# The MLP's down product by Strassen's scheme in a fused RWKV-7 and gelu MLP kernel

## The chip, the cores and the metric

One core of one Trainium2 chip. The metric is device time in microseconds for one execution. Engines are named as in the profile: PE (TensorE's matmuls, PEld its weight loads), DVE (VectorE), ACT (ScalarE), POOL (GpSimd), SP (the queue that issues the DMAs).

## The reference

A linear attention (RWKV-7) over 4 batches, 8 heads, 768 steps and 40 channels gives x of 3072 tokens by 320; behind it stands an MLP with a hidden width of 2048. All in float32 (the MLP's weights come as float64).

```python
for t in range(S):
    y[:, :, t] = np.einsum('bhd,bhde->bhe', rt, state)
    Sa = np.einsum('bhde,bhe->bhd', state, at)
    state_decay = state * wt[:, :, None, :] - np.einsum('bhd,bhe->bhde', Sa, bt)
    state = state_decay + np.einsum('bhd,bhe->bhde', vt, kt)
...
h = x @ w_in                              # 3072 x 320 by 320 x 2048
g = h * (1.0 / (1.0 + np.exp(-1.702 * h)))
return (g @ w_out).astype(np.float32)     # 3072 x 2048 by 2048 x 320
```

## The kernel before

Time is cut into 12 chunks of 64 steps. A chunk has two **units** (each for two of the four batches), 24 in all. A unit's attention is done in chunk form: decays (`decay`), scores (`prep`), the inverse of a triangular matrix in five doubling steps (`inverse`), and the state's read-out and update (`solve`). A step of the inverse goes from PE (`ps_level`) to DVE, which makes E (line 765) and transposes it to ES (line 714), then to ACT, DVE or POOL, which spread ES to EX (lines 719, 721), and back to PE; ACT or DVE copy W out of PSUM beside it (line 763). A unit ends with the decayed read-out "x" (`decayed`, line 965: four multiplies of 128x128 on DVE or POOL) and a way through DRAM that turns it into xT.

When both units of a chunk are done, the chunk's **MLP** (`mlp`) works on its 256 tokens: four quarters q of `up` matmuls (64x256, ps_up), each followed by a `gelu` on ACT (line 1000) that writes the tile g (4 buffers), and two `down` products (p = 0, 1; 128 tokens each) that add up all 16 blocks of the hidden width in one PSUM pair (64x320, ps_down). `store` copies one PSUM bank to ob (ACT or DVE, line 1024), adds the other (DVE, line 1026) and stores. PSUM is four pairs of banks, shared by everything. Every matmul works on a 64x64 quarter of PE's array, and four quarters are in work at once. The weights are turned from float64 to float32 on chip at the start, with a tile `extra` for raw pieces, free afterwards; POOL adds the halves in `joined` (line 475).

The order of everything is a list, `ORDER` (line 109): each token is a task's number, the engine's letter (p, a, d, g, s) and the PSUM pair. `Plan.add` notes what each task must follow, `Plan.listed` reads the list, and each engine works its tasks strictly in that order. Which engine makes an EX, an "x" or a copy is settled there too. In the list as it is, the MLP's matmuls fill PE's queue between the attention's, and lag behind the attention by one to two chunks (xT has three buffers).

Of the kernel before, what the change touches and what calls it, by code (L numbers as in the profile page):

```python
# [58 lines left out]
class Plan:  # L59
# [5 lines left out]
    def add(self, rank, engines, fn, reads=(), uses=(), writes=(), room=(), pair=None, most=None, size=0, release=0.0):  # L65

        t = Task(rank, engines, fn, pair, most, size)
        t.release = release  # L70
        for key in uses:
            self.used.setdefault(key, []).append(t)
        for key in reads:
            t.after.update(self.made[key])
            self.used.setdefault(key, []).append(t)
        for name, n in (*writes, *room):
            if name in self.slots:
                old = (name, n - self.slots[name])
                t.after.update(self.made.get(old, ()), self.used.get(old, ()))
        for key in writes:  # L80
            self.made.setdefault(key, []).append(t)
        if pair is not None:
            writers = self.of_pair.setdefault(pair, [])
            t.after.update(o for o in writers if "PE" in o.engines)
            writers.append(t)
        t.after.discard(t)
        self.tasks.append(t)
# [22 lines left out]
0s 8s 1s4 5s 102a 7s 6s 3a 9s 158a 87p0 88p1 10s 89a1 100p2 90a0 95d 13s4 4a 11s 93d 12s 101d2 98p3 2s 94d 97d 17s 103p1 16s  # L110
96d 143p0 15s 104a1 105d1 142p2 144a0 106d 99d3 107p1 145a2 18s4 149g 132p3 108a1 109d1 156p0 45s4 150d 27s 151g 157d0 159p2
14s4 110p1 160a2 161d2 91s4 130p0 162d 19a 24s4 112d1 163p2 111a1 22d 26s4 25s 164a2 113p1 20d 131a0 153g 165d2 34s4 92a 274s
21d 166p0 114a1 152g 273s 148a 154p2 115d1 275s 167a0 168d0 116p1 23g 28a 155d2 264p0 345s 117d1 265p2 133a3 344s 266a2 118d1
169p3 36s 31d 33s 119p1 278g 170a3 171d3 35s 120d1 42s 122a1 172p2 279d 280g 121a 43s 124d1 123a1 126p3 174d2 125a1 127d3 287a
29d 128p1 173a2 44s4 288p3 30d 54s4 37a 175p2 129d1 32g 51s4 290d3 134p1 179a2 147s4 176d2 146s 267a0 135d1 177a 188p0 291d
136p1 277s4 180a2 268g 61s 38d 189a0 343s 289a3 182p0 39d 186p3 138a1 40d 137a1 178a2 292p1 315d 181a2 139d 183a0 53s4 282g
276s 187a3 184p2 294d1 140s 283p0 293a1 335p3 281d 41g 185d2 334p1 284d0 190p2 336a3 60s4 347s 316p0 191d2 318a0 348d 357a
192p3 349d 317d0 358p2 194a3 346s2 62s 193d3 295p0 337a1 195g 360d2 46a 285p3 361d 319p1 296a0 297d0 351g 320a1 286d3 362p0
196s 271a 350d 141s 352g 298p1 338d 363a0 364d0 321p3 385d 359a2 299a1 300d1 386p0 323p2 197s4 49d 322a3 301p1 387a0 47d 324a2
63s4 365p3 302a1 303d1 325d2 388a0 304p1 366a3 367d3 355p0 353p2 308a1 48d 269s3 209p3 52s3 309a1 307d1 210p3 50g 270s3 64a  # L120
305d1 211p3 354d2 212p3 213p3 356d0 310a1 198p2 306a 214p3 65d 199p2 215p3 72s3 216p3 70s3 272d 55a 311p1 339s3 200p2 69s4
368p0 312a1 66d 201p2 369a0 202p2 58d 470p1 203p2 370d0 471a 475s 204p2 478s 205p2 67d 389p0 479s 472a1 492d 206p2 68g 482s
341a 207p2 371p1 390d0 208a2 217p3 373d1 220p0 221p0 56d 474s4 218p3 485g 71s4 222p0 219a3 473d 81s4 223p0 484d 79s 313p2
224p0 372a1 225p0 226p0 314d2 227p0 342d 374p3 231p1 480s4 378a3 232p1 57d 380a3 326p2 562s4 379a3 59g 228p0 78s4 377a3 327d2
233p1 73a 234p1 229p0 375d3 328p2 376d 230a0 391p3 486g 481s3 329d2 340s4 242p0 531d 392a3 483g 330d2 381p3 235p1 382a3 331d
236p1 393p2 487g 243p0 558s4 394d2 80s4 244p0 395d2 74d 488p3 237p1 489d3 532p2 238p1 75d 533a2 383p3 239p1 534a2 332s4 384d3
240p1 76d 493p2 396p3 496a2 495d2 77g 241a1 245p0 397d3 82a 490p1 559s3 398p3 491d1 476a 560s4 83d 333s 253p1 494d2 497d 254p1
84d 85d 255p1 400d3 86g 561s4 550p2 246p0 705s 399d3 551a 572d 555s 247p0 498d 552a2 554s 401d 499a 256p1 553g 556a 500p3 566d
402s 570p2 567g 501a3 248p0 571d2 502d3 565g 249p0 564d 696p2 563g 257p1 250a0 403s2 251d0 477d 258p1 252s 535p3 259p1 536a3
557d 697a 573p0 537p3 575d0 260p1 576a0 700s4 503d 698a2 611d 504g 538a3 539p2 574d0 261a1 578d 568p3 540a2 704s 404p0 577g  # L130
569d3 579a 405p0 406p0 541d2 787s3 702a 407p0 708s 710d 408p0 580p3 409p0 582d3 410p0 262d1 612p2 411p0 583d 711g 412p0 613d2
413p0 614d2 505p1 709d 584g 414a0 426p2 427p2 506d1 706s2 428p2 507d1 429p2 699d 430p2 581d3 615p1 703d 431p2 616a1 585p0
432p2 586a0 508d 433p2 587d0 434p2 509a 784s2 588d 435p2 589d 448p3 436a2 510p1 590p0 511a1 449p3 592d0 591a0 512d1 263s2
415p2 513d 701s 416p2 593d 514a 785s 417p2 594g 418p2 515p0 419p2 516a0 517d0 595p1 518d 420p2 596a1 597d1 421p2 598d 422p2
519a 599d 423p2 424p2 520p0 425a2 437p1 521d0 438p1 523d0 522g 439p1 524d0 440p1 525d0 441p1 442p1 526d0 527p2 718p0 528a2
443p1 719d0 929s 444p1 720d0 529p2 445p1 721d0 446p1 530d2 600p0 723d 447a1 542p2 722d 724g 603d0 605a0 619p1 604d0 543d2
450p3 620a1 606d0 544p2 621d1 601d0 602d 617p1 707s 546d2 451p3 618a1 783s 712d 547g 713d 607p0 725p1 608a0 452p3 609p0 453p3
548s 610d0 932s 454p3 727d1 726d1 622p0 728d 545d2 729a 775p1 455p3 623d0 780s 776a 549s 756d 730p2 624p0 456d3 457d3 731d2
458s 459p3 777a1 778g 732d2 786s 788g 781a 779s 626d0 460p3 625d0 627g 733d 795p1 835d 734a 461p3 735p2 791g 462p3 628s 736a2
796d1 737d2 716p0 792g 738d 463p3 782d 739g 1011s 920p1 757p2 925s 464p3 717d0 758a2 629s 759a2 790d 465p3 740p0 789d 466p3  # L140
741a0 742d0 921a 797p2 467d3 760p0 1008s 468d3 800a2 923d 652p3 469s 761d0 922a1 653p3 926a 930s 798d2 714p1 799d2 654p3 924s
802d 801g 655p3 934d 803a 656p3 836p0 657p3 715d1 658p3 659p3 837d0 762p2 838d0 927d 660p3 763a2 661p3 764p1 662a3 743d 630p0
744d 928s 631p0 632p0 765d1 804p2 766d1 633p0 805a2 806d2 634p0 807d 635p0 808a 745p3 636p0 748d3 637p0 749d3 839p1 933g 750d3
638p0 840a1 1009s 751d3 639p0 809p2 746d3 935g 640a0 641p1 810d2 642p1 793p3 747a 811d2 674p0 812d 794d3 813a 752p2 643p1
753a2 814p3 644p1 815a3 816d3 754p2 645p1 755d2 646p1 817d 647p1 818a 767p3 841p2 768d3 648p1 842a2 649p1 819p3 650p1 820a3
821d3 769p2 822d 651a1 823d 675p0 771d2 931s 770d2 772g 824p3 936d 676p0 827a3 828a3 942p1 829a3 677p0 1153s 830a3 937d 945a1
773s 663p2 825d3 664p2 943d1 1156s 826a 665p2 944d1 999p3 947d 946g 666p2 1000a 1004s 980d 940p1 948g 667p2 941d1 668p2 774s
669p2 670p2 831p1 671p2 1001a3 1002d 1003s 832d1 672p2 1005a 1013d 678p0 673a2 1006d 833p3 843p1 679p0 834d3 1007s 844d1 938p3
845d1 680p0 939d3 846p2 681p0 847d2 949p1 1012g 682d0 848p3 950a1 683d0 1014d 684s 685p2 849d3 1015g 1010s 850d3 1021p0 1016g
951d1 686p2 1024a0 1232s 851d 1235s 981p3 687p2 982a3 952d 852s 1022d0 983a3 953g 1144p1 1023d0 688p2 1026d 1145a 1149s 1025d  # L150
1027g 984p3 1059d 689p2 1154s 954p0 853s 985a3 1147g 690p2 1158d 1148s 955a0 956d0 986p3 1146a1 957d 1150a 691p2 958d 987a3
1151d 988p0 692p2 989a0 1152s 990d0 959p1 693a2 865p3 960a1 694d2 866p3 961d1 867p3 695s 962d 868p3 963d 1028p0 869p3 1029a0
1030d0 870p3 1031d 1157g 871p3 1159d 1032a 1060p2 872p3 873p3 1061a2 874p3 1062d2 1033p1 875a3 854p0 1035d1 855p0 1036d 856p0
1037d 1063p2 857p0 1064d2 1034a1 858p0 964p3 859p0 965a3 966d3 1038p1 967d 860p0 1039a1 1040d1 861p0 1041d 1017p2 968a 1042g
862p0 1018d2 863p0 969p3 864a0 876p1 970d3 877p1 972d3 971g 1043p2 973d3 878p1 1044a2 974d3 879p1 975d3 880p1 881p1 1045d2
1019p0 1046d 976p3 1047a 882p1 1020d0 1233s 883p1 977a3 1166p2 884p1 1169a2 1167d2 1377s 978p0 885p1 1168d2 898p3 1171d 1170g
886a1 979d0 887p2 1172a 1048p0 991p1 1051a0 888p2 1052a0 992d1 889p2 1053a0 890p2 1054a0 891p2 1049d0 993p1 1050a 1067p0 994d1
# [94 lines left out]
def rwkv7_gelu_quick(ctx: ExitStack, tc: tile.TileContext, time_d, v_d, w_d, wc_d, ak_d, b_d, rv_d, w_in, w_out, out):  # L252
    nc = tc.nc
    H, D, S = 8, 40, out.shape[0] // 4
    DM = H * D
# [731 lines left out]
    def mlp(c):  # L987
# [47 lines left out]
        for p in BITS:  # L1035
            down(p)
# [105 lines left out]
```

## Time and profile before

| | |
|---|---|
| median of 3 runs (lowest to highest) | 682.02 us (680.43 to 682.2) |
| profiled execution, span from first to last instruction | 680.9 us |
| mean granted clock of TensorE | 0.987 (0.79 between 20 and 60 us, else 1.00) |
| matmul records, all / ps_up / ps_down | 19488 / 3840 / 3072 |
| gelu on ACT | 48 of 1024 ns |
| DVE instructions | 912 |
| POOL instructions | 204 |

The profiled execution's time is shown as its span only; one of the runs is shorter than it, so next to nothing lies around it. Busy time of an engine is the union of its instructions' durations. A matmul of float32 stands in the trace as two records, each with a weight load. Group lines give line, engine, operation, tiles (out<-in), count, then durations or busy time; timeline lines give start, length of the merged piece, engine, line, operation and count, so neighbouring pieces' starts give the pace. Wait lines give who waited for whom, the total in us, how often, and the longest.

### The profile page before, as it was taken

What the parts mean: (1) busy time and instruction counts of PE and PEld (TensorE: products, weight loads), DVE (VectorE), ACT (ScalarE), POOL (GpSimd) and SP (SyncE); (2) the same over time, 40 slices, a digit from 0 to 9 for tenths busy, and PEclk for the clock granted to TensorE, in tenths of its full rate; (3) what the DMA queues carried; (4) which work ended last, traced back from release to release, by engine and by line L of the source; (5) the groups of instructions that cost most, each with busy time, mean ns of one, the idle gap of its engine ahead of it and who ended that gap; (6) DMA issues with size and microseconds to landing.
All of it is one profiled execution on the core that took longest, in us unless ns stands there. A gap on an engine that the chain in (4) does not pass through costs nothing.

```text
span 680.9 us, 42186 instructions
## 1 busy us (share of the span) xinstructions
PE 651.5 (96%) x19488; PEld 561.8 (83%) x19488; DVE 452.8 (66%) x912; ACT 328.9 (48%) x682; POOL 175.4 (26%) x204
## 2 busy tenths in 40 slices
PE   5677999999999999999999999999999999999997
PEld 4666998787999788888888898798888799898785
DVE  5686789767867758858776687768666766675001
ACT  3665845644554754574445455455354354262110
POOL 5442345224123223223213221222412320300000
PEclk9977999999999999999999999999999999999999
DMA  7875563415314414432404513513412411200100
GB/s 218 275 245 148 180 203 110 142 42 152 110 36 130 129 33 120 125 115 71 126 13 126 150 38 108 153 35 106 145 33 70 121 53 42 73 13 23 51 12 20
DMA packets 35312, 69.73 MB, mean 102 GB/s; under 512 B 5440, under 2 KB 14656, under 8 KB 35136
## 3 DMA queue, kind: packets, MB, share of 16 engines
q1 hardware_dynamic: 35136, 67.03, 32.7%
q8 instruction: 153, 2.51, 1.5%
q14 instruction: 23, 0.19, 0.1%
HBM read 59.15 MB, written 7.86 MB: 98 GB/s over the span
## 4 chain that ended last, share of the span: by engine, by line
PE 90%; DMA 5%; DVE 2%; ACT 1%; issue 1%; SPq 1%; ACTq 0%; DVEq 0%
PE ps_up L303 30%; PE ps_down L303 30%; PE ps_level L303 8%; PE ps_y L303 5%; PE ps_B L303 4%; PE ps_X L303 3%; PE ps_N L303 2%; PE ps_rz L303 1%; PE ps_RV L303 1%; PE ps_A L303 1%; DMA w_sb<-in_w_in 1%; PE ps_zT L303 1%; PE ps_cum L303 1%; DMA rv<-in_rv 1%; DMA b<-in_b 1%
## 5 line engine op out<-in xcount | busy, mean ns | idle before, releaser
L303 PE MATMUL ps_up<-xT_all,w_sb 64*64 64x256 f32 x3840 | 249.4, 377 | 0.2 <-PE ps_rz L303 0.2
L303 PE MATMUL ps_down<-w_sb,g 64*64 64x320 f32 x3072 | 239.7, 430 | 0.2 <-ACT zr L881 0.2
L303 PEld LDWEIGHTS ps_up<-xT_all,w_sb 64*64 64x64 f32 x3840 | 168.3, 133 | 15.7 <-PE ps_rz L303 0.3
L303 PEld LDWEIGHTS ps_down<-w_sb,g 64*64 64x64 f32 x3072 | 135.5, 133 | 36.7 <-ACT zr L881 0.4
L1000 ACT ACTIVATE g<-ps_up 128x1024 f32<-128x1024 f32 x48 | 49.2, 1024 | 46.1 <-PE ps_up L303 45.6
L721 POOL TENSOR_TENSOR EX<-ES,quads 128x512 f32<-128x512 f32 x30 | 39.7, 1325 | 118.2 <-DVE ES L714 78.4
L763 ACT COPY W<-ps_level 128x512 f32<-128x512 f32 x56 | 32.7, 585 | 66.8 <-PE ps_level L303 65.2
L303 PEld LDWEIGHTS ps_level<-W,EX 64*64 64x64 f32 x2560 | 57.7, 134 | 6.2 <-DVE T L842 0.2
L765 DVE TENSOR_TENSOR E<-two,ps_level 128x256 f32<-128x256 f32 x80 | 33.1, 415 | 34.4 <-ACT W L763 29.7
L303 PE MATMUL ps_level<-W,EX 64*64 64x64 f32 (+1 forms) x2560 | 54.6, 217 | 0.0
L719 ACT ACTIVATE EX<-ES,quads 128x256 f32<-128x256 f32 x82 | 37.2, 501 | 31.7 <-DVE ES L714 31.3
L303 PEld LDWEIGHTS ps_level<-PT,EX 64*64 64x64 f32 x1280 | 32.0, 144 | 12.0 <-DVE EX L735 3.5
L631 POOL TENSOR_TENSOR ak<-ak,FT 128x512 f32<-128x512 f32 x17 | 22.1, 1299 | 76.7 <-DMA ak<-in_ak 49.8
L303 PE MATMUL ps_level<-PT,EX 64*64 64x64 f32 (+2 forms) x1280 | 34.0, 240 | 7.4 <-DVE EX L735 5.0
L714 DVE STREAM_TRANSPOSE ES<-E 128x256 f32<-128x256 f32 x80 | 35.3, 443 | 4.4
L303 PE MATMUL ps_y<-M,bh 64*64 64x104 f32 (+1 forms) x768 | 35.9, 252 | 1.1 <-issue 0.8
L303 PE MATMUL ps_y<-RV,kh 64*64 64x104 f32 (+1 forms) x768 | 36.2, 253 | 0.7 <-DVE M L919 0.5
L903 ACT COPY B<-ps_B 128x416 f32<-128x416 f32 (+1 forms) x35 | 17.2, 492 | 33.4 <-PE ps_B L303 33.2
L303 PEld LDWEIGHTS ps_y<-RV,kh 64*64 64x64 f32 x768 | 29.2, 137 | 3.2 <-DVE M L919 1.3
L919 DVE TENSOR_TENSOR M<-ps_X,later 128x832 f32<-128x832 f32 (+1 forms) x24 | 23.9, 994 | 11.3 <-PE ps_X L303 10.5
L303 PEld LDWEIGHTS ps_y<-M,bh 64*64 64x64 f32 x768 | 27.8, 137 | 1.8 <-issue 1.2
L303 PE MATMUL ps_B<-RV,A 64*64 64x104 f32 (+1 forms) x768 | 28.5, 250 | 0.4 <-issue 0.3
(133 smaller groups left out, 1085.3 us busy)
## 6 DMA issues: line engine op xcount, KB each, us to landing
ak<-in_ak SPq DMA_DIRECT2D x48, 160.0 KB
rv<-in_rv SPq DMA_DIRECT2D x48, 160.0 KB
time<-in_time SPq DMA_DIRECT2D x24, 320.0 KB
xT_all<-x_dram SPq DMA_DIRECT2D x48, 160.0 KB
wc<-in_wc SPq DMA_DIRECT2D x20, 264.0 KB
logw<-in_w SPq DMA_DIRECT2D x24, 160.0 KB
RV<-in_v SPq DMA_DIRECT2D x24, 160.0 KB
b<-in_b SPq DMA_DIRECT2D x48, 80.0 KB
```

Source lines behind the costliest of these rows:

```text
L303: nc.tensor.matmul(o, lhsT, rhs, start=start, stop=True, skip_group_check=True)
L631: plan.add(R, {"DVE": 690.0, "POOL": 1270.0, "sbuf": True}, lambda t: of(t.engine).tensor_mul(ahT(), ahT(), FT_of(i)), reads=T("ak", "FT") ...
L714: plan.add(rank, dve(256), lambda t: nc.vector.transpose(ES(n), source(t)), writes=[key("ES", n, 6)], **reads)
L719: nc.scalar.activation(dst[:, :, h], ES(n), ACT.Copy, scale=quads[:, h, :1])
L721: of(t.engine).tensor_mul(dst, ES(n).unsqueeze(2).to_broadcast([128, 8, 2, 32]), quads.unsqueeze(1).to_broadcast([128, 8, 2, 32]))
L763: plan.add(rank, any2(512), lambda t: copy(t.engine)(tiles_of(W(n + 1)), blocks(psum(t, ""), 64)), writes=[key("W", n + 1, 5)], pair=pair)
L765: plan.add(rank, dve(256), lambda t: nc.vector.tensor_sub(tiles_of(E(n + 1)), every(two32, [128, 2, 4, 32]), blocks(psum(t, ""), 64)[:, :, ...
L903: plan.add(R, any2(4 * wide), lambda t: copy(t.engine)(dst(), some(psum(t, "")[:, :, :208])), writes=[("Bv", i)] if x and c > 0 else T("B" ...
L919: plan.add(R + 1, dve(8 * wide), lambda t: nc.vector.tensor_tensor(M_of(i)[:, :, :wide].rearrange("p (j b) n -> p b j n", b=2), some(psum( ...
L1000: plan.add(-45, {"ACT": 1030.0, "table": "gelu"}, lambda t: nc.scalar.activation(g_of(c * NQ + q).rearrange("p m r n -> p r m n"), psum(t, ...
```

## The change

For chunks 1 to 11 `fast_down` takes the place of `down`; chunk 0 keeps the old one (`CLASSIC = 1`). The chunk's down product is seen as a 2x2 block product: tokens in two halves of 128, hidden blocks in two halves, output columns in two halves of 160. Strassen's scheme in Winograd's form needs seven block products where the plain way needs eight. For each quarter q there are four additions on tiles of 128x256 (S1 to S4, on DVE or POOL; S in four buffers of its own, and g overwritten in place), and 7 products of 8 matmuls of 64x160. The seven sums are kept in three PSUM pairs: x and y with three products each (480 columns), z with one. x and y are evacuated to a tile `sums` (a copy on ACT or DVE, an add on DVE), z is added on its way out, and four combining operations on DVE or POOL make the two output tiles. The sums and differences of weight blocks are formed once, by four subtractions of 128x1280, in the tile `extra`. g has 6 buffers instead of 4, ob 2 instead of 1, and the scratch space for dynamic DMAs is set to 1024 bytes. `ORDER` is new behind chunk 0, which also moves attention tasks in time and between engines: EX from POOL (30 to 6) to ACT and DVE, "x" from POOL (40 multiplies to 4) to DVE (56 to 92). In both programs together with the additions: DVE has 1102 instructions instead of 914, ACT 751 instead of 684, POOL 216 instead of 209, PE 10802 matmuls instead of 9746, SP 414 as before.

```diff
-            t.after.update(o for o in writers if "PE" in o.engines)
+            t.after.update([o for o in writers if "PE" in o.engines][:1 if loose else None])
...
+    CLASSIC = 1
...
-                     A=1, B=1, ... xT=3, g=4, ob=1), 4)
+                     A=1, B=1, ... xT=3, g=6, S=4, sums=1, ob=2), 4)
...
+    w_sums = extra.rearrange("p (k q f n) -> p k q f n", k=4, q=NQ, f=2)
...
+        for k, (one, two) in enumerate(((block(0, 1), block(0, 0)), (block(1, 1), w_sums[:, 0]), (block(0, 1), block(1, 1)), (block(1, 0), w_sums[:, 1]))):
+            plan.add(50, {"DVE": 1500.0, "POOL": 3000.0, "sbuf": True}, lambda t, k=k, one=one, two=two: of(t.engine).tensor_sub(w_sums[:, k], one, two),
...
+        def fast_down():
...
+            def add(q, key, dst, one, two, reads, over=()):
...
+                plan.add(-46, {"DVE": 436.0, "POOL": 750.0, "sbuf": True}, lambda t: of(t.engine).tensor_add(dst(q), one(q), two(q)),
...
+            def product(pair, at, left, right, key, q, also=()):
...
+                    for f in BITS:
+                        for r, b in QUARTERS:
+                            mm(ps[HALF[b], r, 160 * at:160 * at + 160], left(q)[HALF[r], f, b * 64:(b + 1) * 64], right(q)[HALF[r], f],
+                               q == 0 and at == 0 and f == 0)
...
+            for q in range(NQ):
+                add(q, "s1", over, half(1, 0), half(1, 1), ["g"], ["S"])
+                add(q, "s3", half(1, 0), half(1, 0), half(0, 0), ["s1"])
+                product("x", 0, half(0, 0), raw(0, 0), "g", q, sums if q == 0 else [])
+                product("x", 1, over, made(0), "s1", q)
+                product("x", 2, half(1, 0), made(2), "s3", q)
+                add(q, "s2", half(0, 0), half(0, 0), over, ["s1", "s3", "x0"])
+                add(q, "s4", over, half(0, 0), half(0, 1), ["s2", "x1"])
+            for q in range(NQ):
+                product("z", 0, half(0, 1), raw(1, 0), "g", q)
+            for q in range(NQ):
+                product("y", 0, half(1, 1), made(3), "g", q)
+                product("y", 1, half(0, 0), made(1), "s2", q)
+                product("y", 2, over, raw(1, 1), "s4", q)
+            evacuate("x", 0)
+            evacuate("y", 3)
...
+            combine(160, lambda e: e.tensor_sub(total()[:, 4], total()[:, 4], total()[:, 0]), [("wholex", c), ("wholey", c)], [("u", c)])
+            combine(320, lambda e: e.tensor_add(total()[:, 2::4], total()[:, 1:3][:, ::-1], twice(total()[:, 4])), [("u", c)], [("vk", c)])
...
-        for p in BITS:
-            down(p)
+        if c >= CLASSIC:
+            fast_down()
+        else:
+            for p in BITS:
+                down(p)
...
-    nc = bacc.Bacc("TRN2", target_bir_lowering=False, num_devices=1)
+    nc = bacc.Bacc("TRN2", target_bir_lowering=False, num_devices=1, dynamic_dma_scratch_size=1024)
```

## The prediction

> **What bounds the kernel now.** I read the page's first part, then the windows of the body and the end, then TensorE's waits.
>
> ```profile
> PE 651.5 (96%) x19488; PEld 561.8 (83%) x19488; DVE 452.8 (66%) x912; ACT 328.9 (48%) x682; POOL 175.4 (26%) x204
> ```
> ```profile
> 100.00:120.00 20.00, 19.78 (x500) 16.18 (x496) 18.57 (x29) 10.49 (x20) 9.58 (x6) 1.00 0.39 120
> 105.00:620.00 515.00, 513.69 (x15805) 441.64 (x15798) 369.44 (x773) 260.57 (x530) 130.27 (x139) 1.00 0.30 89
> 625.00:676.00 51.00, 51.00 (x900) 40.68 (x892) 4.84 (x14) 4.95 (x6) 0.00 (x0) 1.00 0.11 31
> ```
> The columns behind the length are busy time (and instructions) of PE, PEld, DVE, ACT and POOL, then the granted clock. From 105 us on PE has work without a gap at full clock, DVE is busy 72% of that time, POOL 25%.
>
> ```profile
> PE ps_y L303 <- issue: 0.8, 2, 0.4
> PE ps_down L303 <- ACT zr L881: 0.2, 1, 0.2
> PE ps_up L303 <- PE ps_rz L303: 0.2, 1, 0.2
> ```
> These are all of PE's waits between 105 and 676 us: 1.2 us. So the body is bound by PE, and a microsecond of matmul taken away is won, as long as DVE, ACT and POOL still have their results ready in time. That condition is the whole question, since the change pays for matmuls with vector work.
>
> **What PE gains.** The chain of waits near the end gives clean runs of both MLP products (start, length, matmul records; each matmul of f32 leaves two records), and the timeline a run of narrower ones.
> ```profile
> 628.64 10.78 PE ps_down L303 x160
> 639.42 4.32 PE ps_up L303 x80
> ```
> ```profile
> 305.17 0.56 PE L303 MATMUL ps_B<-RV,A 64*64 64x104 f32 x16
> 305.52 0.57 PE L303 MATMUL ps_B<-zr,ak 40*64 40x104 f32 x16
> 305.88 0.67 PE L303 MATMUL ps_level<-W,EX 64*64 64x64 f32 x32
> ```
> 320 columns: 10.78/160 = 67.4 ns a record; 256: 54.0; 104, from start to start: (0.35 + 0.36)/32 = 22.2. Both steps are 0.209 ns a column, so 160 columns should take 22.2 + 56 x 0.209 = 33.9 ns. A chunk's down product has 3072/12 = 256 records of 320 columns, 17.25 us; seven half-size products (7 x 4 quarters x 8 matmuls x 2) are 448 records of 160, 15.19 us. That is 2.06 us a chunk, **22.7 us** for 11 chunks. Weight loads rise as well (each record has its load, mean 133 ns, four array quarters at once), but the 64-column matmuls pass at about 15 ns a record with the same loads, so loads don't set the pace at 33.9.
>
> **The end.** Before, behind PE's last matmul (676.1) stand one DVE copy, one DVE add and the store:
> ```profile
> 676.11 0.49 DVE L1024 COPY ob<-ps_down 128x320 f32<-128x320 f32 x1 [7.60 <-PE ps_down L303]
> 676.64 0.49 DVE L1026 TENSOR_TENSOR ob<-ob,ps_down 128x320 f32<-128x320 f32 x1
> 677.15 1.11 SPq L333 DMA_DIRECT2D out<-ob  x2
> ```
> In the new order the last y product is followed by four z products (32 matmuls, 64 records, 2.2 us). Meanwhile stand an ACT copy of 480 (estimate 0.57, between its rows of 320 and 512), a DVE add of 480 (0.65), four combining operations (0.33, 0.49, 0.49, 0.33) and z's two adds (0.33 each): about 3.8 us with the gaps between dependent ones. So 1.6 us stand behind PE's end in place of 1.05: **+0.6**. Inside the last chunk the order has ten products or more between the last gelu and the first matmul that needs it, which covers the gelu's 1.02 us.
>
> **What DVE must now do.** Counts are from the order of instructions of both programs. The new order first differs where the matmul work summed along it is 62 us (about 107 us on the clock). The attention units run ahead of the MLP in it: the last unit's read-out stands at 488 of the 607 us of matmul work (before: 583 of 630), and the last 120 us are MLP alone, with DVE under 40% busy. So everything is decided in the **stage** from 60 to 480 us of matmul work. There DVE has 878 instructions in place of 631 for the same 420 us of PE. Sum of durations by the rows: 461 us in place of 330. The additions: 73 Strassen adds, 38 us; evacuations and combinations 24 (less 11 of the old ones); the decayed read-outs "x", 80 instead of 34, since the new order takes them off POOL, 19; EX, taken off POOL too, 11; the four weight sums of 1.5 us (estimate, from the rows of 512), 6; the rest is more attention within the stage.
>
> An add of 128x256 has no row. Nearest are these DVE groups (duration min/median/max); E reads PSUM, the others only SBUF:
> ```profile
> L765 DVE TENSOR_TENSOR E<-two,ps_level x80: 382/420/423, 116.3 to 612.7; 128x256 f32<-128x256 f32 x80
> L709 DVE TENSOR_TENSOR PT<-two,PT x10: 381/400/969, 106.4 to 538.6; 128x256 f32<-128x256 f32 x10
> L965 DVE TENSOR_TENSOR x<-zr,FT x56: 276/282/3027, 47.1 to 630.0; 128x128 f32<-128x128 f32 x56
> ```
> Bounds 0.38 and 0.97; I take 0.52: the median near 0.42, and 0.10 for meeting POOL. That 0.10 is the mean excess over the median of DVE's multiplies, scans and adds with both inputs in SBUF after 80 us (20.6 us in 215 of them). The x of 3027 ns began while POOL's weight addition (2988 ns) ran; E never passes 423. [...]
>
> Durations overlap, though:
> ```profile
> 108.19 0.68 DVE L955 TENSOR_TENSOR zr<-ps_y,zr 128x512 f32<-128x512 f32 x1
> 108.79 0.48 DVE L946 TENSOR_TENSOR zraw<-ps_y,zr 128x320 f32<-128x320 f32 x1
> 109.19 2.49 DVE L416 COPY PT<-one 128x256 f32<-128x256 f32 x2
> ```
> A ready instruction begins 0.08 us before the one ahead of it ends, one that depends on the instruction ahead 0.035 behind it. With 749 free ones (-0.078), 83 dependent and 46 tiny ones (+0.036, +0.013), DVE's occupancy is 461 - 58 + 4 = **407 us against PE's 420**: before it was 299. DVE stops being cover and becomes a second engine that is nearly full: 97%.
>
> What that costs PE I take from blocks. Cut the stage into blocks of equal matmul work; where DVE's occupancy in a block passes PE's, PE waits for the difference. In the old order blocks of 10 us give 1.7 us of such excess and blocks of 5 us 7.4; PE really waited 1.2 us, so 10 us is about what the buffers even out. The new order gives 14.9 us with 10 (26 with 5, 8 with 20, 3 with 60). I take 15, less the 1 that was there: **+14**, ends 2 and 25. ACT (301 us of durations in the stage, before 237) and POOL (130, before 115) stay under three quarters full and I cost them at nothing; DVE's longer queue hides them. The six g, four S and two ob buffers take waits away that PE didn't have: nothing. SP issues as many transfers as before, nothing.
>
> **Sum** against the profiled execution, whose span is 680.9: 680.9 - 22.7 + 0.6 + 14 = 672.8. The median of the runs is 682.0, 1.1 above it, so **674**.
>
> **Rivals.**
> - *Chains make PE wait* (slower). Both orders are fixed, and each step of the inverse goes DVE (E, transpose), ACT, PE, and back; DVE already waits 29.7 us for ACT's W before its E. The adds bring new waits into DVE's queue (s1 for a gelu, s2 and s4 for the x products that still read what they write over), and behind each stand the transposes of two units and the evacuations that free PE's four PSUM pairs. If such waits keep DVE at 90% in the stage, it takes 407/0.90 = 452 us, PE waits 32, and the time is 680.9 - 22.7 + 0.6 + 32 + 1 = 692. It loses against the old kernel below 92% (442 us). For it: the body's mean was 72%, the densest 20 us 18.57 (93%). Against it: between 105 and 120 us DVE was busy 15 of 15 us and PE hardly waited. Chance 0.22.
> - [...] Chance 0.12.
> - *The cover holds*: the buffers even out 60 us and more, PE waits 0 to 5: 660 to 665. Chance 0.13.
> - *The products gain nothing*: half-size matmuls cost 38.5 ns by their loads, and seven times half is the old time: 681 or more. Chance 0.03.
>
> **Numbers.** Forecast (666 to 682) 0.50. A difference under 0.3% (2 us) can't be told from none. Faster: most of the forecast and the cover, 0.54; within 0.3%: 0.12; slower 0.34. From 661 to 693 about two in ten are left out.
>
> **What would show it.** Right: 160-column matmuls near 34 ns a record in runs, a down product of 15.2 us a chunk; DVE over 90% busy between 110 and 540 us; PE's waits there 10 to 20 us in many short ones, released by DVE; an attention that ends some 120 us ahead of the end; adds of 0.5 us in the mean. [...]

## The result, and the profile after

The changed kernel takes 738.1 us (median; 737.1 to 741.7) beside 682.1 for the kernel before: ratio 1.082, 95% interval 1.078 to 1.086. The profiled execution's span is 735.3 us, before 680.9. The prediction said 674 (661 to 693).

First the page's busy times, then the windows (length, then busy time and instructions of PE, PEld, DVE, ACT and POOL, then the granted clock):

```profile
PE 658.3 (90%) x21600; PEld 590.2 (80%) x21600; DVE 516.1 (70%) x1100; ACT 357.9 (49%) x749; POOL 165.6 (23%) x211
```
```profile
100.00:120.00 20.00, 18.11 (x525) 14.05 (x520) 15.34 (x30) 13.20 (x26) 8.10 (x5) 1.00 0.52 156
105.00:610.00 505.00, 457.10 (x15992) 404.97 (x15988) 399.37 (x878) 275.00 (x580) 120.82 (x144) 0.99 0.31 90
610.00:720.00 110.00, 110.00 (x2601) 100.79 (x2597) 35.33 (x88) 18.48 (x21) 0.52 (x1) 1.00 0.08 19
```
From 105 us to the end of attention (610 us) PE has holes, at a granted clock of 0.99, and DVE is busy 79% of that time, where it was 72% before. Behind it, from 610 to 720 us, PE is busy without a gap. TensorE's waits from 105 us on, where before there were three lines with 1.2 us:

```profile
PE ps_level L320 <- issue: 9.6, 13, 1.5
PE ps_down L320 <- issue: 7.3, 13, 1.0
PE ps_rz L320 <- issue: 5.4, 6, 2.1
PE ps_up L320 <- issue: 4.4, 5, 1.7
```
"Issue" means that PE waited for nothing that the profile can name: neither DVE nor ACT nor a transfer. These are the four largest of the list; the waits stand ahead of many kinds of matmul alike. Over the whole list "issue" comes to 39.3 us, ACT to 4.1 and DVE to 2.7.

What does the stage lose? I count a matmul record as 0.2083 ns a column and 0.35 ns, 14.6 ns at least (the pace of this case's runs; twice that on a 64x128 tile of PE's array, below), call the sum **work** and the rest of the time **lost**. A **gap** is a distance of more than 240 ns between the starts of two matmul records that follow each other, counted less 60 ns. "Late" are the gaps that end 1.15 to 1.62 us after a packet of the instruction queue has landed (below).

```
                        105 us to the end of attention         then to PE's end
                        length  work   lost  (late, gaps)      length  work
before                  523     518.5    4.9  ( 3.2,  12)       47      47.1
after                   505     421.3   83.2  (55.1,  66)      120     119.2
```
All the matmul work of the kernel is 629.8 us before and 607.1 after, 22.7 less, as the prediction has it. The stage got 18 us shorter though 97 us of work left it, and 72 of these 97 now stand behind it.

The instruction queue on the page brings 16,384-byte packets (2.79 MB in 170). The line after, then before (packets, MB, share):

```profile
q8 instruction: 170, 2.79, 1.6%
q8 instruction: 153, 2.51, 1.5%
```
I take a packet for 128 matmul records and their 128 loads, 256 instructions: in runs of matmuls alone PE stops after exactly 128 records (below). Then the 21,600 records after would fill 168.75 packets and the 19,488 before 152.25, and the page has 170 and 153. The experiments' kernels fit as well, from 14,880 records in 117 packets to 24,352 in 191. So PE's program comes in blocks of some 128 records, and a gap can be set beside the landing of a block. One stretch of the timeline and the landings in it (from the trace's transfers):

```profile
252.93 0.66 PE L320 MATMUL ps_down<-extra,g 64*64 64x160 f32 x8
254.58 0.36 PE L320 MATMUL ps_down<-extra,g 64*64 64x160 f32 x3 [0.99 <-issue]
```
```
block on its way   landed    next matmul behind a gap    after landing   gap
247.76             248.90    250.20                      1.30            0.61
252.03             253.32    254.58                      1.26            1.29
255.82             257.22    258.57                      1.35            1.35
```
(The table's gaps are full distances between starts.) PE stops in the middle of one row of like matmuls that wait for nothing (8, then 3), and goes on 1.3 us after the block has landed. Of the 129 gaps of the stage (75.7 us) 66 (55.1 us) are of this kind; gaps that had nothing to do with the blocks would fall into that window of 0.47 us about one time in eight, since blocks land 3.9 us apart (median; a quarter of the intervals under 3.72). In the kernel before it is 12 of 113, as chance would have it. The late gaps also keep step with the blocks: 39 of the 65 distances from one to the next are 126 to 128 matmul records, and 21 more are two to seven times that; the three above stand 127 records apart. In the kernel before none of the 11 distances fits. In the stage after, 128 records take 3.38 us of work; before, 4.13.

### The profile page after: what moved, and what is told of

Same layout as the page of the kernel before. It is cut to its first block, busy times and chain, and to the rows that moved or that the text cites. A ratio compares the mean times of both kernels' runs of the same rounds, so it can differ in the third digit from the quotient of the medians.

```text
span 735.3 us, 46662 instructions
## 1 busy us (share of the span) xinstructions
PE 658.3 (90%) x21600; PEld 590.2 (80%) x21600; DVE 516.1 (70%) x1100; ACT 357.9 (49%) x749; POOL 165.6 (23%) x211
## 3 DMA queue, kind: packets, MB, share of 16 engines
q8 instruction: 170, 2.79, 1.6%
## 4 chain that ended last, share of the span: by engine, by line
PE 76%; DVE 8%; issue 8%; ACT 5%; DMA 2%; SPq 0%; ACTq 0%; DVEq 0%
PE ps_up L320 24%; PE ps_down L320 24%; PE ps_level L320 8%; PE ps_y L320 5%; PE ps_B L320 4%; PE ps_X L320 2%; PE ps_RV L320 2%; PE ps_N L320 1%; PE ps_rz L320 1%; PE ps_A L320 1%; ACT Tc L834 1%; DVE ES L739 1%; PE ps_zT L320 1%; PE ps_Q L320 1%; ACT PT L821 1%
## 5 line engine op out<-in xcount | busy, mean ns | idle before, releaser
L320 PEld LDWEIGHTS ps_up<-xT_all,w_sb 64*64 64x64 f32 x3840 | 163.7, 133 | 27.8 <-issue 7.3
L320 PE MATMUL ps_down<-extra,g 64*64 64x160 f32 x2112 | 98.1, 299 | 2.8 <-issue 2.8
L320 PE MATMUL ps_down<-w_sb,g 64*64 64x160 f32 (+1 forms) x1664 | 84.7, 319 | 3.0 <-issue 2.4
L1025 ACT ACTIVATE g<-ps_up 128x1024 f32<-128x1024 f32 x48 | 48.8, 1024 | 68.4 <-PE ps_up L320 67.9
L320 PEld LDWEIGHTS ps_down<-extra,g 64*64 64x64 f32 x2112 | 77.7, 134 | 5.3 <-issue 4.6
L744 ACT ACTIVATE EX<-ES,quads 128x256 f32<-128x256 f32 x112 | 50.5, 501 | 39.0 <-DVE ES L739 36.0
L320 PEld LDWEIGHTS ps_down<-w_sb,g 64*64 64x64 f32 x1664 | 62.4, 134 | 7.8 <-issue 3.1
L1064 DVE TENSOR_TENSOR S<-g 128x256 f32<-128x256 f32 x70 | 32.1, 470 | 50.0 <-ACT g L1025 38.3
L320 PE MATMUL ps_level<-W,EX 64*64 64x64 f32 (+1 forms) x2560 | 59.4, 220 | 7.4 <-issue 5.2
L834 ACT COPY Tc<-ps_level 32x64 f32<-32x64 f32 x114 | 23.0, 202 | 35.0 <-PE ps_level L320 17.6
L320 PE MATMUL ps_down<-extra,S 64*64 64x160 f32 x704 | 34.6, 298 | 1.8 <-issue 1.8
```

The costliest lines, as they stand in the source:

```text
L320: nc.tensor.matmul(o, lhsT, rhs, start=start, stop=True, skip_group_check=True)
L744: nc.scalar.activation(dst[:, :, h], ES(n), ACT.Copy, scale=quads[:, h, :1])
L834: copy(t.engine)(dst, src[:, u, :, f])
L1025: plan.add(-45, {"ACT": 1030.0, "table": "gelu"}, lambda t: nc.scalar.activation(g_of(c * NQ + q).rearrange("p m r n -> p r m n"), psum(t, ...
L1064: plan.add(-46, {"DVE": 436.0, "POOL": 750.0, "sbuf": True}, lambda t: of(t.engine).tensor_add(dst(q), one(q), two(q)), reads=[(x, n) for ...
```

## The experiments

All kernels but the two of the last experiment ran once. The kernel before took 677.9 to 688.9 us in the 23 runs beside those two, so differences of a few us between single runs decide nothing.

Theory F: PE's instructions arrive too slowly. A block of 128 records takes 3.5 to 3.9 us to come, whatever is in it, so matmuls too narrow and too close together wait for the next block. Theory D, the prediction's own: VectorE's additions set the pace. A third, O, came up on the way: attention itself, in this order, can't go faster.

### Narrow matmuls without Strassen's scheme

```diff
-                        for r, b in QUARTERS:
+                        for n, (r, b) in product((0, 160), QUARTERS):
                             o = p * 128 + b * 64
-                            mm(po[HALF[b], r, :DM], g[...], w_out_sb[HALF[r], f * DM:(f + 1) * DM], f == 0)
+                            mm(po[HALF[b], r, n:n + 160], g[...], w_out_sb[HALF[r], f * DM + n:f * DM + n + 160], f == 0 and n == 0)
```


> The kernel before, with each 320-column matmul of the down product split into two of 160 columns: the same columns through PE, 22560 matmul records in place of 19488, no vector work added and the old order. Theory F (PE's instructions arrive in blocks of 256, with at least some 3.5 us from one block to the next, and dense stretches run out of them): PE gets waits that nothing in the profile releases, and the time goes to 700 to 740 us. Theory D (the new kernel's PE waits for vector work and its chains): no change, 680 to 686 us.

Measured: 740.7 beside 685.2, 0.7 above F's range. The kernel before, with its order, its engines' work and its columns unchanged, is as slow as the changed kernel as soon as its down matmuls are half as wide and twice as many. TensorE's waits from 105 to 690 us:

```profile
PE ps_down L303 <- issue: 22.7, 31, 1.6
PE ps_B L303 <- issue: 3.3, 4, 1.5
```
It loses 60.6 us in its stage, 48.0 of it late (68 of 75 gaps), with 3.57 us of work in 128 records. F holds; nothing of D's is in this kernel.

### The additions taken out, the products made wider, and both

```diff
-                plan.add(-46, {...}, lambda t: of(t.engine).tensor_add(dst(q), one(q), two(q)),
+                plan.add(-46, {...}, lambda t: None,
```


> The changed kernel without the Strassen additions of gelu blocks; the products read the plain blocks instead, PE's stream is unchanged (output differs). About 60 us of DVE and 29 us of POOL go, and so do PE's waits for the adds. F: 715 to 738 us, as before this edit or little less. D: 665 to 695 us.

```diff
-                    for f in BITS:
-                        for r, b in QUARTERS:
-                            mm(ps[HALF[b], r, 160 * at:160 * at + 160], left(q)[HALF[r], f, b * 64:(b + 1) * 64], right(q)[HALF[r], f],
+                    for r, b in QUARTERS:
+                        mm(ps[HALF[b], r, o:o + 320], left(q)[HALF[r], 0, b * 64:(b + 1) * 64], w[HALF[r]], q == 0 and at == 0)
```


> The changed kernel with its seven products as 4 matmuls of 320 columns each in place of 8 of 160: the same columns through PE, half the instructions for them (19136 records in all), all vector work, waits and the order as in the changed kernel. It leaves out half of the hidden blocks and multiplies the others by twice the columns, so its output is another one. F: 660 to 690 us, and the waits without a releaser go. D: 730 to 740 us.

The third kernel has both edits:

> Both edits of the last two kernels together: products of 320 columns and no additions (output differs). Both theories: 658 to 675 us; what stays above 659 is the new order's own. If F holds, the step from the wide kernel to this one is the price of the adds: 0 to 20 us. If D holds, it is most of the 70 us.

```
                             us      records   length  work   lost  (late)
changed kernel               738.1   21600     505     421.3  83.2  (55.1)
without additions            742.4   21600     510     422.7  87.1  (61.1)
wide products                713.4   19136     481     419.4  62.0  (34.1)
both                         709.4   19136     477     418.0  59.4  (36.2)
```
The kernel without additions is 4 us above what F expected and far above D's range: nothing is won without them, so D falls as the cause of this loss. Where products are wide the additions come to 4 us, too little for single runs to tell. Half as many product matmuls are worth 25 to 33 us, a clear but small answer. F expected more: 59 to 62 us stay lost although these kernels have fewer records than the kernel before, which loses 5, and only 34 to 36 of them are late. Something else seems to hold the stage near 480 us.

### Wider tiles: the same columns in fewer records

```diff
-                        for r, b in QUARTERS:
-                            mm(ps[HALF[b], r, 160 * at:160 * at + 160], left(q)[HALF[r], f, b * 64:(b + 1) * 64], right(q)[HALF[r], f],
+                        for r in BITS:
+                            mm(ps[:, r, 160 * at:160 * at + 160], left(q)[HALF[r], f], right(q)[HALF[r], f],
```


> The changed kernel with each product matmul on a 64x128 tile of PE's array instead of two on 64x64: the same products, sums and order, half the instructions for the products (19136 records in all), with the full Strassen work and its result. F: the time of the kernel with products of 320 columns, 705 to 720 us. If weight loads of 128 columns don't hide behind matmuls of 160 columns, it is slower than that: 740 us and more.

The next has the same edit in the up product as well, and the third both in the kernel before:

> The same with the up product on 64x128 tiles as well (17216 records in all). F: dense stretches get longer pauses between blocks from the MLP, 675 to 700 us. D: nothing changes against the changed kernel, 730 to 740 us.

> The kernel before with up and down on 64x128 tiles (16032 records in place of 19488). Its PE had no waits after 105 us, so F expects little: 675 to 683 us. Slower than 686 would say that the wider tiles cost something by themselves.

Measured: 733.3, 747.7 and 773.4, beside 685.4, all above what F expected. The late part does fall, from 55.1 to 19.2 and 9.4 us in the first two, yet the three stages lose 73.9, 89.1 and 97.2. The timeline of the third shows why (64*128 is the tile of PE's array):

```profile
302.87 1.35 PE L303 MATMUL ps_down<-w_sb,g 64*128 64x320 f32 x8
304.15 0.69 PE L303 MATMUL ps_level<-W,EX 64*64 64x64 f32 x32
304.78 1.35 PE L303 MATMUL ps_down<-w_sb,g 64*128 64x320 f32 x8
```
Eight records of 134.8 ns (twice the 67.4 on 64x64) are 1.08 us, but 1.28 pass until the next kind begins; 32 of 14.6 ns are 0.47, but 0.63 pass. A change of tile there and back costs about 0.36 us here, and 272 of them are 98 us: the 97 lost. The first two kernels' stages have 102 and 222 of them, some 34 and 76 us by the starts of their records. A way out of late instructions, but not where attention's matmuls on 64x64 lie between.

### Runs of matmuls alone

```diff
+    runs = [("m64", QUARTERS, 64, 64, 64), ("m104", QUARTERS, 64, 64, 104), ("m160", ...), ("m320", ...), ("h160", ..., 64, 128, 160), ("f160", ..., 128, 128, 160)]
+    for s, (name, places, K, M, N) in enumerate(runs):
...
+        for n in range(128):
+            for r, b in places:
...
+                mm(ps[cols, r, :N], w_sb[rows, ...], w_sb[rows, 2048:2048 + N], True)
```


> The kernel before, and behind its last task six runs of 128 sets of matmuls that wait for nothing: 64x64 tiles with 64, 104, 160 and 320 columns (1024 records each), 64x128 tiles with 160 (512 records), 128x128 with 160 (256 records). F: PE alone takes a block of 256 instructions (128 records) in no less than some 3.4 us, so the run of 64 columns takes about 27 us instead of 15, 104 columns about 27 instead of 23, while 160 (35) and 320 (69) go at their columns' pace. If instructions come fast enough, all four go at 0.21 ns a column. The wide tiles: 64x128 at 34 us for its 128 sets if weight loads hide, 128x128 longer if they don't.

Six runs of independent matmuls behind the kernel before, with nothing else at work. The timeline:

```profile
680.69 2.10 PE L303 MATMUL ps_m<-w_sb 64*64 64x64 f32 x128 [1.65 <-issue]
684.16 2.10 PE L303 MATMUL ps_m<-w_sb 64*64 64x64 f32 x128 [1.38 <-issue]
...
706.36 3.08 PE L303 MATMUL ps_m<-w_sb 64*64 64x104 f32 x128 [0.39 <-issue]
709.83 3.08 PE L303 MATMUL ps_m<-w_sb 64*64 64x104 f32 x128 [0.39 <-issue]
713.58 3.08 PE L303 MATMUL ps_m<-w_sb 64*64 64x104 f32 x128 [0.66 <-issue]
...
724.26 106.02 PE L303 MATMUL ps_m<-w_sb 64*64 64x104 f32 x2126 [0.39 <-issue]
830.21 35.04 PE L303 MATMUL ps_h<-w_sb 64*128 64x160 f32 x512
865.18 35.04 PE L303 MATMUL ps_f<-w_sb 128*128 128x160 f32 x256
```
Here are the stops by themselves: with 64 columns exactly 128 matmul records, then an idle 1.38 to 1.65 us, then the next 128. The starts are 3.47 to 3.75 us apart (once 4.02, where 64 columns pass into 104), for 64 and for 104 columns alike: 27.0 and 29.1 ns a record, as F expected. The transfers show the round: PE starts a block at 680.69, the next block's transfer begins at 681.86 and lands at 682.81, and PE starts that block at 684.16; the one behind it follows in the same way, at 685.22, 686.57 and 687.91. In these two rounds the next transfer begins 1.17 and 1.06 us after PE has begun a block, and lands 0.02 and 0.31 us behind that block's end (682.79, 686.26): nothing lay ready in this run to even out a dense stretch. 128 records of 160 columns are 4.4 us, longer than the 3.47 to 3.75 from block to block, and that run (with the 320s inside the merged piece of 106 us) has no such stop: 34.4 ns a record, 67.4 for 320. Wide tiles keep the pace by column: 68 ns on 64x128, 136 on 128x128.

### The up product in matmuls of 512 columns

```diff
-                ph, x = psum(t, "ps_up"), xT_of(c)[:, :, k]
-                for r, h in QUARTERS:
-                    mm(ph[HALF[h], r, m * 256:(m + 1) * 256], w_in_sb[HALF[r], 2 * q + m, k, h * 64:(h + 1) * 64], x[HALF[r]],
+                ph, x = psum(t, "ps_up"), xT_all[:, c % 3, 128 * k:128 * k + 512]
+                for r, h in QUARTERS if m == 0 else ():
+                    mm(ph[HALF[h], r], w_in_sb[HALF[r], 2 * q, k, h * 64:(h + 1) * 64], x[HALF[r]], k == 0)
```


> e4_no_adds_wide (no Strassen additions, products in half as many matmuls) with the up projection issued in matmuls of 512 columns instead of 256, so 17,216 matmuls instead of 19,136 for the same columns; the output differs because the additions are left out and rows are taken from the wrong halves. e4 took 709.4 us and lost 59 us between 105 us and the end of attention. Theory F (TensorE's instructions arrive too slowly where narrow matmuls lie close together): the wide matmuls now leave room, the loss falls to 20 to 40 us, 670 to 690 us. Rival O (the new order has its own chains of waits, whatever the number of instructions): the loss stays near 59 us, 703 to 712 us.

> e2_after_wide320 (additions kept, products in half as many matmuls) with the up projection in matmuls of 512 columns; 17,216 matmuls, the output differs for the same rows. Theory F: 20 to 40 us below e2's 713.4, and within 6 us of the kernel beside it without additions. Theory D (VectorE's additions set the pace once instructions do not): 12 us or more above the kernel without additions.

> The kernel before with its up projection in matmuls of 512 columns: 17,568 matmuls instead of 19,488, the same columns; the output differs because rows are taken from the wrong halves. Theory F: the kernel before loses only 3 us to late instructions, so 678 to 686 us beside 682 to 686. If wide matmuls were worth something by themselves (fewer loads, fewer starts), it would be 670 us or below, and the two runs beside it would have to be read against that.

Measured: 729.8, 730.4 and 721.6, beside 687.4. All three miss, and the control shows that the edit was a bad one: the kernel before itself loses 42 us with it. The matmuls of a task with m = 1 are done in the task with m = 0, so PE's queue has long pieces of MLP in one place and none in another. There its waits have names:

```profile
PE ps_level L303 <- ACT EX L719: 8.9, 7, 1.6
PE ps_X L303 <- DVE T L842: 2.0, 2, 1.1
PE ps_level L303 <- POOL EX L721: 1.6, 1, 1.6
```
Of instructions this tells nothing. It does tell that attention's chains reach PE as soon as the MLP's matmuls between its steps are missing. The two with and without additions agree within 0.6 us, so nothing here speaks for D either.

### How fast can attention go?

```diff
-                for r, h in QUARTERS:
+                for r, h in QUARTERS if k == 0 else ():
                     mm(ph[HALF[h], r, m * 256:(m + 1) * 256], ...
...
-                    for f in BITS:
+                    for f in BITS[:1]:
                         for r, b in QUARTERS:
                             mm(ps[HALF[b], r, 160 * at:160 * at + 160], ...
```


> The changed kernel with only a fifth of the up matmuls (one of five pieces of the sum) and half of the product and down matmuls, every wait, every other engine's work and the order left as they are; the output differs. 15,936 matmuls, about 250 us of TensorE work less. It asks what attention in the new order takes without the work between. Theory F (the loss beside late instructions is small): the stage from 105 us to the end of attention shrinks from 505 us to 370 to 410 us, the pace of 128 matmuls per 3.5 to 3.75 us. Rival O (attention's own chains in the new order set a floor near 470 us, which is why the runs with half as many product matmuls stopped at 477 to 481 us): the stage stays at 450 us or more.

> The kernel before with the same cut, a fifth of the up matmuls and half of the down matmuls, 14,880 matmuls; the output differs. Theory F: the stage shrinks from 523 us to about the same 370 to 410 us as the changed kernel's. Rival O: the old order's chains are shorter, so its stage is 40 us or more below that of the changed kernel cut in the same way.

Measured: 639.0 and 601.5. The windows of the changed kernel cut so, then of the kernel before:

```profile
105.00:570.00 465.00, 347.49 (x12240) 284.70 (x12237) 393.62 (x873) 272.91 (x580) 123.46 (x144) 0.88 0.34 97
```
```profile
105.00:570.00 465.00, 364.46 (x12132) 276.05 (x12136) 359.89 (x769) 254.43 (x524) 128.17 (x136) 0.93 0.33 96
```
The stages last 470 and 465 us, with only 259 and 291 us of matmul work. Neither theory had it: there is a floor as O said, but it is no property of the new order. With 163 us of work gone the new order's stage is 35 us shorter; with 228 gone the old one's is 58 us shorter. PE's waits have names now (the kernel before, cut, then the largest of the changed kernel, cut):

```profile
PE ps_level L303 <- ACT EX L719: 20.3, 20, 2.9
PE ps_y L303 <- DVE M L919: 4.9, 4, 1.7
PE ps_level L303 <- DVE EX L721: 4.8, 7, 1.6
```
```profile
PE ps_level L320 <- DVE EX L746: 9.6, 7, 2.9
```
The lines of ps_level and EX are the round of the inverse (PE, DVE, then ACT or DVE, PE). Over the whole lists DVE releases 45 us of PE's waits and ACT 34 in the kernel before cut so; in the changed kernel cut so DVE releases 65, ACT 25, and "issue" stands for 22. DVE is busy 85% of that stage, so behind late instructions stands a second limit in which DVE has the largest part, near to the prediction's rival of chains. The floor holds some slowness of these two kernels' own: the granted clock fell to 0.88 and 0.93, and "issue" has 22 and some 13 us of PE's waits. So 465 to 470 is an upper bound for it at full clock. It would fit the kernels with wide products, which stopped at 477 and 481; that it is what stopped them is not shown.

### Strassen's scheme only behind attention

CLASSIC is set to 11 (chunk 11 alone) or 10 (chunks 10 and 11); the order is that of the kernel before, with the last chunks' down matmuls replaced.

```diff
-    CLASSIC = 1
+    CLASSIC = 11
```


> Strassen's scheme for chunk 11 alone, which lies behind the end of attention; chunks 0 to 10 and the order of everything ahead as in the kernel before, the four weight sums formed on VectorE after the last attention step. Theory F (the products are worth what their columns say where instructions are not short): 256 matmuls of 67.4 ns become 448 of 34.4 ns, 1.8 us less, up to 0.8 us of it given back by the longer end of sums; 680.4 to 682 where the kernel before takes 682 to 683, ratio 0.997 to 0.999. Rival: the products gain nothing anywhere, because their loads or additions set their pace: ratio 1.000 or above.

> The same for chunks 10 and 11; chunk 10's products stand where its down matmuls stood, among and behind the last steps of attention, its additions between VectorE's last attention operations. Theory F: twice the gain of one chunk, 2.5 to 3.6 us less than the kernel before, ratio 0.995 to 0.997, if the shorter filler still covers the last steps of attention. Rival: the additions ahead of those steps and the lost cover take it back: 1 to 4 us slower than the kernel with the last chunk alone.

Measured: 683.2 beside 683.0, ratio 1.0013 (0.998 to 1.0046), and 680.3, ratio 0.9967 (0.993 to 1.0004). Matmul work falls from 629.8 to 627.7 and 625.6 us, 2.1 a chunk, and the last kernel's tail is 44.5 us long with 43.5 of work. The first kernel's profile has a gap of 1.3 us "issue" in its tail, behind no landing, that would take most of its gain; it can't be told from no change, and so decides nothing. By the medians the second is 2.9 us faster than the first, not 1 to 4 us slower as its rival had it, though their runs overlap (678.9 to 687.1 and 679.9 to 686.2). It is 2 to 3 us faster than the kernel before, close to what F said; but its interval just takes in no change, so I don't call it faster.

## Why the prediction was wrong

The step that failed is "What that costs PE I take from blocks": **+14** for PE's waits. The loss grew by 78 us (83.2 less 4.9). With 78 in place of 14 the sum is 680.9 - 22.7 + 0.6 + 78 = 737, where the span was 735.3. The blocks compared PE's work with DVE's alone; the number of instructions that PE must be sent had no term at all, and the releasers' chains were left to a rival. Step by step:

- **PE's gain, 22.7**: right. Work fell by 22.7, and the 160-column run of the experiment takes 34.4 ns a record, where 33.9 was worked out. But it could be had only where nothing else held PE up.
- **The end, +0.6**: right. The last DVE add ends 1.4 us behind PE's last matmul of the changed kernel, where 1.6 was said.
- **The price of an addition, 0.52**: too high. The groups' mean is 0.47, 0.46 and 0.42 us, 0.05 and less above their medians (0.42), where 0.10 was taken for meeting POOL. The 125 additions in whose time POOL had no operation on a tile took 0.40 to 0.43 us; the 12 others took 0.42 to 1.52, 0.82 in the mean:

```profile
L1064 DVE TENSOR_TENSOR S<-g 128x256 f32<-128x256 f32 x70 | 32.1, 470 | 50.0 <-ACT g L1025 38.3 <-PE ps_down L320 9.8 <-POOL g L1064 0.8
L1064 DVE TENSOR_TENSOR g<-g,S 128x256 f32<-128x256 f32 x35 | 16.0, 461 | 21.4 <-PE ps_down L320 20.8
L1064 DVE TENSOR_TENSOR g<-g 128x256 f32<-128x256 f32 x32 | 13.3, 418 | 0.4
```
- **DVE's occupancy of the stage, 407**: nearly right in time (399 busy), wrong in share: 79% of a stage of 505 us, not 97% of 420. The question put to the trace, whether DVE keeps up with PE, was not the one that decided. Without the additions the kernel is no faster.
- **"Loads don't set the pace at 33.9", since 64-column matmuls pass at 15 ns**: true of the loads (34.4 ns a record in the run of 160 columns), but the row of 64 columns was one of 32 records. In a run of 1024 the same matmuls stop every 128 records, at 27.0 ns a record. The count of matmuls had a price of its own that the prediction did not look for: 11% more records in the whole, 128 of them in 3.38 us of work in the stage where it was 4.13. The page's instruction queue (153 packets in 680.9 us, one per 4.45) stood there to be asked.
- **The tail**: "the last 120 us are MLP alone" came true to the microsecond, and it should have warned. Work of 72 us was moved behind attention on the assumption that attention can end that much earlier. In the cut kernels its stage took 465 to 470 us even with 259 and 291 us of work in it. With 105 us ahead and 120 + 5.6 behind, a floor of 470 alone would give about 700 us.
- **Rivals**: chains (692) has the right sign and perhaps a part of the cause, but not by the additions, and DVE was busy 79%, not 90%. That "the products gain nothing" for the loads' sake was nearest in mechanism, the matmuls' number as a price, and had a chance of 0.03. The list of signs had no line for waits without a releaser, which is what came.

How much of the 78 is which? The late gaps are 52 more than before, and the same narrowing of matmuls in the old order, whose stage lies well above the floor, costs 56: that late instructions cost tens of us is shown. The stage needs up to 49 us more than its work if 470 is its floor. These overlap, since "issue" is also a part of PE's waits in the cut kernels (22 and some 13 us); I can't divide the rest between them, and its cause stays open. Narrow matmuls alone make the old order slower. A floor alone would make the new order slower than the kernel before if it lies above 450 us (681 less 105 and 125.6), which the upper bounds leave open.

## What to carry to other kernels

Count the instructions that an engine must be sent, not only their time: here PE gets 128 float32 matmul records in 3.5 to 3.9 us, so by these runs a change that makes matmuls narrower wins nothing below some 27 to 30 ns a record, and that over each block of 128, not in the mean of a stage (the changed kernel's stage had 3.38 us of work to 128 records in the mean, and the split kernel's still lost 60.6 us with 3.57). Before work is moved out of a stage, take most of it out as an experiment and see whether the stage gets shorter at all. And a long run of an operation in isolation (1024 records, not 32) shows limits that the short runs inside a kernel hide.

## What the runs showed of the hardware

- PE's instructions come in packets of 16,384 bytes, some 128 matmul records and as many loads each (170 packets for 43,200 instructions after, 153 for 38,976 before). Packets are on their way for 1.0 to 1.1 us in the median and land 3.40 to 3.88 us apart when PE is starved in runs of matmuls alone, 3.9 in the median of the changed kernel's stage; PE goes on 1.3 to 1.6 us behind a landing in the runs alone. In the runs of 64 columns it was idle for 1.38 to 1.65 us in every 3.47 to 3.75.
- A change of PE's tile between 64x64 and 64x128 costs about 0.36 us there and back (the timeline of the wide tiles).
- The granted clock was 0.88 and 0.93 in the cut kernels' windows, where PE was busy 75% and 78% of the time, and 0.99 and 1.00 in the full ones, where it was busy 91% and all but 100%.
